# A one-token decode layer on one NeuronCore: the order of work written out, with weight chunks between the links of attention

## The chip, the cores and the metric

The kernel runs on 1 of the 8 cores of one Trainium2 chip. The metric is the time of one execution on the device in microseconds (us), the median of several runs. A core has a matrix engine (PE, with its weight loads listed apart as PEld), a vector engine (DVE), a scalar engine (ACT), a general engine (POOL) and a sync engine (SP), which here only issues DMAs. Each engine works through its own instructions in the order in which the program gives them, and waits where an instruction needs another engine's result. Sixteen DMA engines carry the data from the chip's memory into the core's own memory.

## The reference

One token `x` (1 x 1024) is normalised, and three things are added: `x` itself, attention over a window of 4096 cached keys and values (32 query heads that share 4 key/value heads), and a gated feed-forward layer. All is float32.

```python
def _A_ref(x, k_cache, v_cache, wq, wo):
    ...
    q = (lambda x, *d: x.transpose(*d))((x @ wq).reshape(B, Sq, Hq, Dh), 0, 2, 1, 3)
    k = jnp.repeat(k_cache[:, :, Sk - W:, :], rep, axis=1)
    v = jnp.repeat(v_cache[:, :, Sk - W:, :], rep, axis=1)
    scores = jnp.einsum("bhqd,bhkd->bhqk", q, k) * (Dh ** -0.5)
    p = _softmax(scores, axis=-1)
    o = jnp.einsum("bhqk,bhkd->bhqd", p, v)
    return (lambda x, *d: x.transpose(*d))(o, 0, 2, 1, 3).reshape(B, Sq, Hq * Dh) @ wo

def _B_ref(x, w_gate, w_up, w_down):
    g = jnp.einsum("bsd,df->bsf", x, w_gate)
    u = jnp.einsum("bsd,df->bsf", x, w_up)
    h = _gelu(g) * u
    return jnp.einsum("bsf,fd->bsd", h, w_down)
...
xn = _layernorm(x, axis=-1)
return x + _A_ref(xn, A_k_cache, A_v_cache, A_wq, A_wo) + _B_ref(xn, B_w_gate, B_w_up, B_w_down)
```

`wq` is 1024 x 4096, `wo` 4096 x 1024, `w_gate` and `w_up` 1024 x 3584, `w_down` 3584 x 1024. Every weight and every cached row in the window is read once, 94.4 MB in all, so the kernel is a stream of data with a little work on each piece.

## The kernel before

**The stream.** `items` is a list of 23 chunks: four of `wq` ("q"), then "k" 0, "g" 0 (`w_gate`), "v" 0, "g" 1 to 3, "k" 1, "u" 0 (`w_up`), "v" 1, "u" 1 to 3, four of `wo` ("o") and four of `w_down` ("d": eight tiles in each of the first three chunks, four in the last). A "k" or "v" chunk holds two key/value heads. `load(n)` takes one of the four buffers of the pool `stream` and issues the chunk's DMAs on SP's queue. The first four loads come ahead of all work; the load of chunk n+4 is written behind the work on chunk n, and waits on SP until every reader of that chunk's buffer is done. The last two chunks come in pieces (`TAIL`).

**The work on a chunk.** `project` (chunks q, g, u) multiplies each of a chunk's two rows by its element of `x` and adds it to `part` on DVE (`add_scaled`: line 191 for the first row of a matrix, line 193 for the others). At the end of a matrix, PE adds the 128 partitions of `part` together: `queries` for q, `projected` for g and u (line 212). `transpose_keys` turns a head's keys around with 32 PE transposes in eight groups of four (line 256), each group copied out by ACT to `kT` (line 257; two PSUM buffers alternate). `scores` multiplies (line 265), takes the maximum on DVE (`m`, line 268; `negm`, line 269) and the exponentials on ACT (line 271). `values` transposes the probabilities (lines 284 and 287) and multiplies with v (line 295; copied to `o_sb` on ACT, line 299). `maxima`, `factors`, `normalizers` and `heads` bring the four groups' maxima and sums together over a chain of small steps between PE, DVE and ACT (lines 308 to 354); its end is `oz`, the vector that `wo` is multiplied with. `gelu` (lines 365 to 371) and `hidden` (lines 375 and 376) do the same service for `w_down` and end in `hz`.

**The two output matrices.** `contract` walks over the tiles (128 rows x 1024) of a chunk of `wo` or `w_down`. Most go to DVE, which adds the scaled tile to `out_part` (line 193). The tiles in `ALONE`, 4 of the 32 of `wo` and 10 of the 28 of `w_down`, go to PE, four quarters of 256 columns each, into `out_p` (`accumulate`, line 384). Ahead of tile 26 of `w_down` (`MERGE`) PE adds `out_part` to `out_p`, so every DVE tile must be finished there; tiles 26 and 27 follow on PE. Then DVE adds `x` (line 448) and the result is stored.

**The order.** `tc.manual_schedule()` keeps the order of the program text on every engine. It comes from one loop over `items`: all work of chunk n, then the load of chunk n+4, then the work of chunk n+1. So in chunk "k" both heads' transposes and scores stand together, and the next weight chunk stands behind them in DVE's queue; `factors` stands behind `project` of u 1, `normalizers` and `heads` (as one piece) behind that of u 2, and `hidden` behind `projected("u")` and ahead of the tiles of o 0. In chunk "k" 1 the transposes of head 2 stand ahead of `projected("g")` and `gelu`.

Of the kernel before, what the change touches and what calls it, by code (L numbers as in the profile page):

```python
# [9 lines left out]
F32 = mybir.dt.float32  # L10
AF = mybir.ActivationFunctionType
# [4 lines left out]
P = 128  # L16
D = 1024
# [4 lines left out]
DF = 3584  # L22
NJ = D // (2 * P)
NB = 512
CO = D // 4
CF = DF // 4
TD = DF // P
GROUP = 8

TAIL = {0: 1, 1: 4}  # L30


ALONE = {"o": (0, 8, 16, 24), "d": (8, 12, 16, 18, 20, 22, 24, 25, 26, 27)}
MERGE = ("d", 26)
# [7 lines left out]
def tile_decode_layer(  # L42
# [28 lines left out]

    def grouped(w, a):
        return w[P * GROUP * a:min(P * GROUP * (a + 1), w.shape[0]), :].rearrange(
            "(p t) n -> p t n", p=P
        )

# [3 lines left out]
    items += [("o", a) for a in range(HQ // GROUP)]  # L80
    items += [("d", a) for a in range(-(-TD // GROUP))]
    source = {
        "q": lambda i: [paired(wq, i)], "g": lambda i: [paired(w_gate, i)], "u": lambda i: [paired(w_up, i)],
        "k": lambda i: [window(k_cache, 2 * i + g) for g in range(2)],
        "v": lambda i: [window(v_cache, 2 * i + g) for g in range(2)],
        "o": lambda i: [grouped(wo, i)], "d": lambda i: [grouped(w_down, i)],
    }
    loaded = {}

    def load(n):  # L90
        kind, i = items[n]
        chunk = stream.tile([P, STREAM], F32, name="chunk")
        at = 0
        for src in source[kind](i):
            size = math.prod(src.shape[1:])
            dst = chunk[:, at:at + size]
            at += size
            if len(src.shape) == 3:
                dst = dst.rearrange("p (t n) -> p t n", t=src.shape[1])
            step = TAIL.get(len(items) - 1 - n)  # L100
            if step:
                for t in range(0, src.shape[1], step):
                    cuts = 2 if n == len(items) - 1 and t == src.shape[1] - 1 else 1
                    for cut in range(cuts):
                        cols = slice(cut * D // cuts, (cut + 1) * D // cuts)
                        nc.sync.dma_start(dst[:, t:t + step, cols], src[:, t:t + step, cols])
            else:
                nc.sync.dma_start(dst, src)
        loaded[kind, i] = chunk
# [90 lines left out]

    def project(kind, jj, count):
        if jj == 0:
            part[kind] = work.tile([P, 8 * NB], F32, name="part", tag="part")
        w = loaded.pop((kind, jj))
        n = count * NB
        for r in range(2):
            add_scaled(
                part[kind][:, :n], w[:, r * n:(r + 1) * n], xz[:, r, jj, 0:1], jj == 0 and r == 0
            )

    def add_up(kind, c, at, w):
        nc.tensor.matmul(acc[kind][32 * c:32 * c + 32, at], unit, w, start=True, stop=True)  # L212


    def queries():
        acc["q"] = psum.tile([P, 2 * NB], F32, name="acc_q", tag="acc")
        w = part["q"].rearrange("p (h c s) -> p h c s", c=4, s=32)
        for b in range(2):
            for c in range(4):
                add_up("q", c, slice(b * NB, (b + 1) * NB), w[:, 16 * b:16 * b + 16, c, :])  # L220
# [4 lines left out]
        nc.vector.tensor_copy(  # L225
            qz[:, :, 0:REP], qT[:, :, 0].rearrange("p (g h) -> p g h", g=HKV)
        )

    def projected(kind):
        acc[kind] = psum.tile([P, 2 * NB], F32, name="acc_" + kind, tag="acc")
        full = DF // D * D
        w = part[kind][:, :full].rearrange("p (a c s i) -> p a c i s", a=DF // D, c=4, i=GROUP)
        rest = part[kind][:, full:DF].rearrange("p (c s i) -> p c i s", c=4, s=32)
        for c in range(4):
            add_up(kind, c, slice(0, NB), w[:, 0:2, c])
        for c in range(4):
            add_up(kind, c, slice(NB, NB + D // 4), w[:, 2, c])
        for c in range(4):  # L240
            add_up(kind, c, slice(NB + D // 4, DF // 4), rest[:, c])

# [59 lines left out]
    top = work.tile([HKV, 4, 32], F32, name="top")  # L302
    weight = work.tile([P, HKV], F32, name="weight")
    sel = same.rearrange("p c h -> p (c h)")

# [9 lines left out]
    def factors():  # L315
        mm_p = small("mm_p")
        nc.tensor.transpose(mm_p[:, :HKV], top.rearrange("g c h -> g (c h)"), ident[:HKV, :HKV])
        d = work.tile([P, HKV], F32, name="d")
        nc.vector.tensor_sub(d, m, mm_p[:, :HKV])
        e = work.tile([P, HKV], F32, name="e")  # L320
        nc.scalar.activation(e, d, AF.Exp, scale=SCALE)
        le = work.tile([P, HKV], F32, name="le")
        nc.vector.tensor_mul(le, l, e)
        return e, le

    def normalizers(e, le):
# [4 lines left out]
        nc.vector.tensor_mul(weight, e, r)  # L331

    def heads():
        w_p = small("w_p")
# [4 lines left out]
        for g in range(HKV):  # L339
            nc.scalar.activation(o_sb[:, g], o_sb[:, g], AF.Copy, scale=weight[:, g:g + 1])  # L340


        ot_p = small("ot_p")
        for c in range(4):
            nc.tensor.matmul(  # L345
                ot_p, pick[:, REP * c:REP * c + REP, :].rearrange("p h s -> p (h s)"),
                o_sb[:, :, c, :], start=(c == 0), stop=(c == 3),
            )
        own = work.tile([P, HKV, 16, 8], F32, name="own", tag="rows")
        nc.vector.tensor_mul(  # L350
# [8 lines left out]

    g_sb = work.tile([P, CF], F32, name="g_sb", tag="gate")  # L360
    h_sb = work.tile([P, CF], F32, name="h_sb")

    def gelu():
        t_sb = work.tile([P, CF], F32, name="t_sb", tag="rows")
        nc.scalar.activation(g_sb, acc["g"][:, :CF], AF.Copy)  # L365
        nc.vector.tensor_mul(t_sb, g_sb, g_sb)  # L366
# [7 lines left out]
    def hidden():  # L374
        nc.vector.tensor_mul(h_sb, g_sb, acc["u"][:, :CF])
        nc.vector.transpose(hz.rearrange("p t s -> p (t s)"), h_sb)


    out_p = psum.tile([P, CO], F32, name="out_p", tag="out")
    out_part = None  # L380

# [5 lines left out]

    def contract(kind, a, z, count):
        nonlocal out_part
        if kind == "o" and a == 0:  # L390
            out_part = work.tile([P, D], F32, name="out_part", tag="keys")
        w = loaded.pop((kind, a))
        for i in range(min(GROUP, count - GROUP * a)):
            t = GROUP * a + i
# [3 lines left out]
            if t in ALONE[kind]:  # L398
                accumulate(z[:, t, :], wt, kind == "o" and t == 0, kind == "d" and t == count - 1)
            else:  # L400
                add_scaled(out_part, wt, z[:, t, 0:1], kind == "o" and t == 1)

    ahead = 4
    for n in range(ahead):
        load(n)
    layer_norm()
    state = None
    for n, (kind, i) in enumerate(items):
        if kind == "q":
            project("q", i, 8)  # L410
        elif kind == "k":
            kn = loaded.pop(("k", i))
            half = STREAM // 2
            transpose_keys(2 * i, kn[:, :half])
            if i == 0:
                queries()
            else:
                projected("g")
                gelu()
            scores(2 * i)  # L420
            transpose_keys(2 * i + 1, kn[:, half:])
            scores(2 * i + 1)
        elif kind == "v":
            vn = loaded.pop(("v", i))
            half = STREAM // 2
            values(2 * i, vn[:, :half])
            values(2 * i + 1, vn[:, half:])
            if i == 1:
                maxima()
        elif kind in "gu":  # L430
            project(kind, i, DF // NB)
            if (kind, i) == ("u", 1):
                state = factors()
            elif (kind, i) == ("u", 2):
                normalizers(*state)
                heads()
        elif kind == "o":
            if i == 0:
                projected("u")
                hidden()  # L440
            contract("o", i, oz, HQ)
        else:
            contract("d", i, hz, TD)
        if n + ahead < len(items):
            load(n + ahead)

# [26 lines left out]
```

## Time and profile before

| | |
|---|---|
| time, median of 3 runs | 247.78 us (246.86 to 248.16) |
| the profiled execution: its time | 248.12 us |
| the profiled execution: its span (first to last instruction) | 246.3 us |
| read from memory | 94.38 MB |
| busy: DVE, PE, ACT | 173.8, 77.3, 35.9 us |

The span is what the views of the trace cover; the 1.8 us beside it is start and end of the execution. Below, the time is written from the start of the span. A row of the timeline gives start, duration, engine, line, operation, what is written and read with its shape, how many instructions are taken together, and in brackets how long the engine sat idle ahead of it and what ended that. A row of the windows gives a stretch, its length, the busy time (with the number of instructions) of PE, PEld, DVE, ACT and POOL, then the clock that PE was granted (1.00 is full), the share of the DMA engines and GB/s.

### The profile page before, as it was taken

The page shows a single profiled execution, that of the slowest core. Times are in us where ns is not written, and L with a number is a line of the kernel's source. Part 1 is how long each engine was busy: PE and PEld are TensorE (multiplying, and loading weights), DVE is VectorE, ACT ScalarE, POOL GpSimd, SP SyncE. Part 2 cuts the span into 40 slices and gives each one's busy share as a digit, 9 for nine tenths or more (in the row PEclk, how much of TensorE's full clock was granted, in tenths as well). Part 3 has the DMA queues.
Part 4 walks back from the last instruction along what each step waited for, and adds up shares of the span by engine and source line. Part 5 has one row for each costly group of instructions (what it writes and reads, how often), then busy time and mean ns, then how long its engine had stood idle before and what let it go on. Part 6 is the DMA issues. An engine that isn't in the chain of part 4 may idle for free.

```text
span 246.3 us, 1319 instructions
## 1 busy us (share of the span) xinstructions
PE 77.3 (31%) x492; PEld 38.8 (16%) x492; DVE 173.8 (71%) x128; ACT 35.9 (15%) x63; POOL 0.7 (0%) x6
## 2 busy tenths in 40 slices
PE   1000000395496100495296400370611000335004
PEld 1000000351362000342263100220200000101001
DVE  6285988932209999905419699229499999999990
ACT  2000000161644000153443100400000000000000
POOL 1000000000000000000000000000000000000000
PEclk9999999997779855599677955575695555557555
DMA  7999999999999999999999999999997999996000
GB/s 278 442 458 436 426 431 394 434 449 416 428 454 410 419 447 414 432 427 422 449 418 430 447 433 434 426 426 426 431 426 277 426 404 426 407 376 263 0 0 1
DMA packets 4782, 94.47 MB, mean 384 GB/s; under 512 B 540, under 2 KB 552, under 8 KB 1192
## 3 DMA queue, kind: packets, MB, share of 16 engines
q1 hardware_dynamic: 4760, 94.38, 90.2%
q8 instruction: 4, 0.07, 0.1%
q14 instruction: 2, 0.02, 0.0%
q10 hardware_dynamic: 16, 0.01, 0.0%
HBM read 94.38 MB, written 0.00 MB: 383 GB/s over the span
## 4 chain that ended last, share of the span: by engine, by line
DVE 43%; DMA 24%; PE 24%; ACT 5%; issue 2%; ACTq 0%; DVEq 0%
DVE out_part L193 24%; DMA chunk<-in_A_k_cache 19%; DVE part L193 11%; PE kt_p L256 9%; DMA chunk<-in_A_wq 5%; PE o_p L295 3%; PE s_p L265 3%; PE ot_p L345 2%; DVE m L268 2%; ACT p L271 2%; PE acc_u L212 1%; PE acc_g L212 1%; PE pt_p L284 1%; PE out_p L384 1%; DVE part L191 1%
## 5 line engine op out<-in xcount | busy, mean ns | idle before, releaser
L193 DVE SCALAR_TENSOR_TENSOR part<-chunk,xz,part 128x3584 f32<-128x3584 f32 (+1 forms) x21 | 86.7, 4128 | 5.0 <-DMA chunk<-in_A_wq 4.2
L256 PE MATMUL kt_p<-ident,chunk 128*128 128x128 f32 x128 | 25.0, 364 | 72.0 <-DMA chunk<-in_A_k_cache 61.0
L193 DVE SCALAR_TENSOR_TENSOR out_part<-chunk,oz,out_part 128x1024 f32<-128x1024 f32 x27 | 34.7, 1285 | 1.0
L256 PEld LDWEIGHTS kt_p<-ident,chunk 128*128 128x128 f32 x128 | 19.6, 187 | 79.7 <-DMA chunk<-in_A_k_cache 40.2
L257 ACT ACTIVATE kT<-kt_p 128x512 f32<-128x512 f32 x32 | 18.7, 597 | 68.2 <-PE kt_p L256 67.7
L193 DVE SCALAR_TENSOR_TENSOR out_part<-chunk,hz,out_part 128x1024 f32<-128x1024 f32 x18 | 23.1, 1285 | 0.6
L268 DVE TENSOR_REDUCE m<-s_p 128x1 f32<-128x1024 f32 x4 | 4.9, 1223 | 23.0 <-PE s_p L265 23.0
L384 PE MATMUL out_p<-chunk,hz 128*32 128x256 f32 x80 | 9.3, 609 | 27.8 <-DMA chunk<-in_B_w_down 27.8
L265 PE MATMUL s_p<-kT,qz 128*32 128x512 f32 x64 | 9.1, 694 | 2.6 <-DVE qz L225 2.6
L191 DVE TENSOR_SCALAR part<-chunk,xz 128x3584 f32<-128x3584 f32 (+1 forms) x3 | 6.5, 2169 | 4.5 <-DMA chunk<-in_A_wq 4.5
L295 PE MATMUL o_p<-chunk,pT 128*32 128x512 f32 x64 | 8.4, 644 | 4.1 <-ACT pT L287 4.1
L384 PEld LDWEIGHTS out_p<-chunk,hz 128*32 128x32 f32 x80 | 3.0, 155 | 34.3 <-issue 24.9
L345 PE MATMUL ot_p<-o_sb,pick 128*128 128x512 f32 x8 | 6.0, 917 | 2.8 <-ACT o_sb L340 2.8
L350 DVE TENSOR_TENSOR own<-ot_p,low 128x512 f32<-128x512 f32 x1 | 0.7, 692 | 8.6 <-PE ot_p L345 8.6
L212 PE MATMUL acc_u<-part,unit 128*32 128x512 f32 (+2 forms) x24 | 3.4, 718 | 9.7 <-DVE part L193 9.7
L366 DVE TENSOR_TENSOR t_sb<-g_sb 128x896 f32<-128x896 f32 x1 | 1.1, 1094 | 7.6 <-ACT g_sb L365 7.6
L384 PE MATMUL out_p<-chunk,oz 128*32 128x256 f32 x32 | 2.8, 447 | 10.1 <-DMA chunk<-in_A_wo 10.1
L271 ACT ACTIVATE p<-s_p,negm 128x1024 f32<-128x1024 f32 x4 | 4.5, 1114 | 8.9 <-DVE negm L269 8.9
L384 PE MATMUL out_p<-out_part,unit 128*32 128x256 f32 x8 | 1.1, 635 | 14.5 <-DVE out_part L193 14.5
L284 PE MATMUL pt_p<-ident,p 128*128 128x128 f32 x32 | 5.2, 317 | 0.0
L224 DVE STREAM_TRANSPOSE qT<-q_sb 128x1024 f32<-128x1024 f32 x1 | 1.2, 1245 | 5.2 <-ACT q_sb L222 5.2
L284 PEld LDWEIGHTS pt_p<-ident,p 128*128 128x128 f32 x32 | 4.1, 162 | 4.0 <-issue 4.0
(86 smaller groups left out, 51.1 us busy)
## 6 DMA issues: line engine op xcount, KB each, us to landing
chunk<-in_A_wq SPq DMA_DIRECT2D x4, 4096.0 KB, 30.8
chunk<-in_A_wo SPq DMA_DIRECT2D x4, 4096.0 KB, 22.4
chunk<-in_B_w_gate SPq DMA_DIRECT2D x4, 3584.0 KB, 16.6
chunk<-in_B_w_up SPq DMA_DIRECT2D x4, 3584.0 KB, 15.1
chunk<-in_A_k_cache SPq DMA_DIRECT2D x4, 2048.0 KB, 26.0
chunk<-in_A_v_cache SPq DMA_DIRECT2D x4, 2048.0 KB, 23.6
chunk<-in_B_w_down SPq DMA_DIRECT2D x2, 4096.0 KB
chunk<-in_B_w_down SPq DMA_DIRECT2D x2, 2048.0 KB, 12.1
```

The source lines that it names most:

```text
L191: nc.vector.tensor_scalar(total, w, factor, None, op0=ALU.mult)
L193: nc.vector.scalar_tensor_tensor(total, w, factor, total, op0=ALU.mult, op1=ALU.add)
L212: nc.tensor.matmul(acc[kind][32 * c:32 * c + 32, at], unit, w, start=True, stop=True)
L256: nc.tensor.transpose(t_p[:, jj * P:(jj + 1) * P], kn[:, j * DH:(j + 1) * DH], ident)
L257: nc.scalar.activation(kT[:, i, :], t_p, AF.Copy)
L265: nc.tensor.matmul(s_p[32 * c:32 * c + 32, b, :], qz[:, g, :], kT[:, i, :], start=True, stop=True)
L268: nc.vector.reduce_max(m[:, g:g + 1], s_p, axis=AX.XY)
L271: nc.scalar.activation(p, s_p, AF.Exp, bias=negm[:, g:g + 1], scale=SCALE, accum_out=l[:, g:g + 1])
L284: nc.tensor.transpose(t_p[:, jj * P:(jj + 1) * P], p[:, b, jj * P:(jj + 1) * P], ident)
L295: nc.tensor.matmul(o_p[32 * jj:32 * jj + 32, :, :], pT[:, b, jj].rearrange("p c h -> p (c h)"), v[:, b, jj], start=(b == 0), stop=(b == 1),)
L345: nc.tensor.matmul(ot_p, pick[:, REP * c:REP * c + REP, :].rearrange("p h s -> p (h s)"), o_sb[:, :, c, :], start=(c == 0), stop=(c == 3),)
L384: nc.tensor.matmul(out_p[32 * c:32 * c + 32, :], z, w[:, c * CO:(c + 1) * CO], start=start, stop=stop)
```

## The change

The loop over `items` is gone; every step is written out, with the loads at stated places. Chunks, buffers (four) and the order of the loads stay.

- **Order.** `queries` comes ahead of the transposes of head 0. g 0 is projected between `scores(0)` and the transposes of head 1, u 0 between `scores(2)` and the transposes of head 3. `projected("g")` and `gelu` come ahead of the transposes of head 2. `maxima` stands behind `scores(3)`, `factors` between the values of heads 2 and 3. `project` can take one row of a chunk: the first row of u 1 stands between `factors` and `normalizers`, the second row of u 1 and the first of u 2 between `scaled` (the first part of the old `heads`) and `heads` (its rest). The DVE tiles of o 0 stand ahead of `hidden`.
- **Tiles.** `w_down` is now four chunks of seven tiles (`DOWN`). Eight tiles (`WIDE`) go to PE in two halves of 512 columns into a new PSUM tile `wide_p`, which takes the place of `o_p`; nine (`QUARTERS`) go to PE in quarters as before. DVE keeps 27 of `wo` and 16 of `w_down` (28 and 18 before). `narrow`, behind chunk d 1, adds `wide_p` to `out_part` in two DVE operations on 32 partitions x 512.
- **Sums.** `projected` adds 8 blocks of 448 columns in place of 12 of 512, 256 and 128; `gelu` and `hidden` work on the same 896 columns, held as 2 x 448.
- **Pieces.** Chunks o 3, d 1 and d 2 come in two pieces, d 3 in six, the last of these in two halves (`PIECES`).

```diff
+PIECES = {("o", 3): (4, 4), ("d", 1): (3, 4), ("d", 2): (3, 4), ("d", 3): (2, 1, 1, 1, 1, 1)}
+WIDE = [("o", 0), ("o", 4), ("o", 8), ("o", 16), ("o", 24), ("d", 0), ("d", 7), ("d", 10)]
+QUARTERS = [("d", t) for t in (14, 16, 18, 20, 22, 24, 25, 26, 27)]
 MERGE = ("d", 26)
...
-        w = part[kind][:, :full].rearrange("p (a c s i) -> p a c i s", a=DF // D, c=4, i=GROUP)
...
+        w = part[kind][:, :DF].rearrange("p (a c s i) -> p a c i s", a=TD // DOWN, c=4, i=DOWN)
+        for b in range(2):
+            for c in range(4):
+                add_up(kind, c, (b, slice(0, CF)), w[:, 2 * b:2 * b + 2, c])
...
+            if (kind, t) in WIDE:
+                if (kind, t) == WIDE[0]:
+                    wide_p = psum.tile([P, NB], F32, name="wide_p", tag="o")
+                for c in range(2):
+                    nc.tensor.matmul(
+                        wide_p[32 * c:32 * c + 32, :], z[:, t, :], wt[:, c * NB:(c + 1) * NB],
+                        start=(kind, t) == WIDE[0], stop=(kind, t) == WIDE[-1],
+                    )
+            elif (kind, t) in QUARTERS:
+                accumulate(z[:, t, :], wt, (kind, t) == QUARTERS[0], (kind, t) == QUARTERS[-1])
...
+    def narrow():
+        for c in range(2):
+            rows, cols = slice(32 * c, 32 * c + 32), slice(c * NB, (c + 1) * NB)
+            nc.vector.tensor_add(out_part[rows, cols], out_part[rows, cols], wide_p[rows, :])
...
+    for _ in range(4):
+        load_next()
     layer_norm()
+    for i in range(NJ):
+        project("q", i)
+        load_next()
+    queries()
+    transpose_keys(0, cache("k", 0))
+    scores(0)
+    project("g", 0)
+    transpose_keys(1, cache("k", 1))
+    scores(1)
+    load_next()
+    load_next()
+    values(0, cache("v", 0))
+    values(1, cache("v", 1))
+    load_next()
+    for i in range(1, NJ):
+        project("g", i)
+        load_next()
+    projected("g")
+    gelu()
+    transpose_keys(2, cache("k", 2))
+    scores(2)
+    project("u", 0)
+    transpose_keys(3, cache("k", 3))
+    scores(3)
+    load_next()
+    load_next()
+    maxima()
+    values(2, cache("v", 2))
+    factors()
+    values(3, cache("v", 3))
+    load_next()
+    project("u", 1, (0,))
+    normalizers()
+    ot_p = scaled()
+    project("u", 1, (1,))
+    load_next()
+    project("u", 2, (0,))
+    heads(ot_p)
+    project("u", 2, (1,))
+    load_next()
+    project("u", 3)
+    load_next()
+    projected("u")
+    contract("o", 0)
+    hidden()
+    load_next()
+    for a in range(1, HQ // GROUP):
+        contract("o", a)
+        load_next()
+    for a in range(TD // DOWN):
+        contract("d", a)
+        if a == 1:
+            narrow()
```

More of the change, by code (lines that the diff above doesn't have):

```diff
@@ L99, in load @@
                 dst = dst.rearrange("p (t n) -> p t n", t=src.shape[1])
[L100 to L107, printed above, removed]
+            t = 0
+            for step in PIECES.get((kind, i), ()):
+                cuts = 2 if n == len(items) - 1 and t + step == DOWN else 1
+                for cut in range(cuts):
+                    cols = slice(cut * D // cuts, (cut + 1) * D // cuts)
+                    nc.sync.dma_start(dst[:, t:t + step, cols], src[:, t:t + step, cols])
+                t += step
+            if t == 0:
                 nc.sync.dma_start(dst, src)
@@ L199, in tile_decode_layer, with project @@
     acc, part = {}, {}
-    def project(kind, jj, count):
-        if jj == 0:
+    def project(kind, jj, rows=(0, 1)):
+        if jj == 0 and rows[0] == 0:
             part[kind] = work.tile([P, 8 * NB], F32, name="part", tag="part")
-        w = loaded.pop((kind, jj))
-        n = count * NB
-        for r in range(2):
+        w = loaded[kind, jj]
+        n = HQ * DH if kind == "q" else DF
+        for r in rows:
             add_scaled(
@@ L211, in add_up @@
     def add_up(kind, c, at, w):
-        nc.tensor.matmul(acc[kind][32 * c:32 * c + 32, at], unit, w, start=True, stop=True)
+        nc.tensor.matmul(acc[kind][(slice(32 * c, 32 * c + 32), *at)], unit, w, start=True, stop=True)
     def queries():
@@ L231, in projected @@
     def projected(kind):
-        acc[kind] = psum.tile([P, 2 * NB], F32, name="acc_" + kind, tag="acc")
-        full = DF // D * D
-        w = part[kind][:, :full].rearrange("p (a c s i) -> p a c i s", a=DF // D, c=4, i=GROUP)
[L235 to L241, printed above, removed]
+        acc[kind] = psum.tile([P, 2, NB], F32, name="acc_" + kind, tag="acc")
+        w = part[kind][:, :DF].rearrange("p (a c s i) -> p a c i s", a=TD // DOWN, c=4, i=DOWN)
+        for b in range(2):
+            for c in range(4):
+                add_up(kind, c, (b, slice(0, CF)), w[:, 2 * b:2 * b + 2, c])
     m = work.tile([P, HKV], F32, name="m")
@@ L303, in tile_decode_layer @@
     weight = work.tile([P, HKV], F32, name="weight")
+    e = work.tile([P, HKV], F32, name="e")
+    le = work.tile([P, HKV], F32, name="le")
     sel = same.rearrange("p c h -> p (c h)")
@@ L348, in heads @@
             )
+        return ot_p
+    def heads(ot_p):
         own = work.tile([P, HKV, 16, 8], F32, name="own", tag="rows")
@@ L357, in heads @@
         )
-    g_sb = work.tile([P, CF], F32, name="g_sb", tag="gate")
-    h_sb = work.tile([P, CF], F32, name="h_sb")
+    g_sb = work.tile([P, 2, CF], F32, name="g_sb", tag="gate")
+    h_sb = work.tile([P, 2, CF], F32, name="h_sb")
     def gelu():
-        t_sb = work.tile([P, CF], F32, name="t_sb", tag="rows")
-        nc.scalar.activation(g_sb, acc["g"][:, :CF], AF.Copy)
+        t_sb = work.tile([P, 2, CF], F32, name="t_sb", tag="rows")
+        nc.scalar.activation(g_sb, acc["g"][:, :, :CF], AF.Copy)
         nc.vector.tensor_mul(t_sb, g_sb, g_sb)
@@ L386, in accumulate, with contract @@
             )
[L388 to L394, printed above, removed]
+    def contract(kind, a):
+        nonlocal out_part, wide_p
+        size, z = (GROUP, oz) if kind == "o" else (DOWN, hz)
+        w = loaded[kind, a]
+        for i in range(size):
+            t = size * a + i
             wt = w[:, i * D:(i + 1) * D]
@@ L397, in contract @@
                 accumulate(unit, out_part, False, False)
-            if t in ALONE[kind]:
-                accumulate(z[:, t, :], wt, kind == "o" and t == 0, kind == "d" and t == count - 1)
-            else:
[L401 to L405, printed above, removed]
-    layer_norm()
[L407 to L445, printed above, removed]
@@ new lines, in contract @@
+            if (kind, t) in WIDE:
[5 more added lines that the diff above has]
+                        start=(kind, t) == WIDE[0], stop=(kind, t) == WIDE[-1],
+                    )
+            elif (kind, t) in QUARTERS:
+                accumulate(z[:, t, :], wt, (kind, t) == QUARTERS[0], (kind, t) == QUARTERS[-1])
+            else:
+                first = out_part is None
+                if first:
+                    out_part = work.tile([P, D], F32, name="out_part", tag="keys")
+                add_scaled(out_part, wt, z[:, t, 0:1], first)
```

41 lines of the change are left out of this document (23 added, 18 removed).

## The prediction

> **What bounds the kernel now.** I read the slices of the page first, then two stretches of the windows, then the waits, then DVE's timeline.
>
> ```profile
> DVE  6285988932209999905419699229499999999990
> DMA  7999999999999999999999999999997999996000
> GB/s 278 442 458 436 426 431 394 434 449 416 428 454 410 419 447 414 432 427 422 449 418 430 447 433 434 426 426 426 431 426 277 426 404 426 407 376 263 0 0 1
> 130.00:180.00 50.00, 18.42 (x98) 7.57 (x102) 34.42 (x21) 6.05 (x13) 0.00 (x0) 0.66 1.00 431
> 225.00:240.00 15.00, 0.64 (x8) 0.16 (x8) 14.61 (x12) 0.00 (x0) 0.00 (x0) 0.60 0.05 20
> ```
>
> Data flows at about 431 GB/s until the 37th slice of 6.16 us. Then for 15 us (225 to 240) hardly a byte moves, while DVE is full (14.61 of 15 us). So the end is a backlog on DVE. It arose earlier: the slices 9 to 11 and 18 to 27 show holes in DVE while data kept coming. Four groups of waits make most of the holes:
>
> ```profile
> DVE m L268 <- PE s_p L265: 23.0, 3, 10.5
> DVE own L350 <- PE ot_p L345: 8.6, 1, 8.6
> DVE t_sb L366 <- ACT g_sb L365: 7.6, 1, 7.6
> DVE h_sb L375 <- PE acc_u L212: 3.6, 1, 3.6
> ```
>
> (us in total, times, longest.) These are DVE's links in attention's chains, with the next weight chunk queued behind them.
>
> ```profile
> 97.03 7.94 DVE L193 SCALAR_TENSOR_TENSOR part<-chunk,xz,part 128x3584 f32<-128x3584 f32 x2 [0.30 <-DMA chunk<-in_B_w_gate]
> 166.40 7.93 DVE L193 SCALAR_TENSOR_TENSOR part<-chunk,xz,part 128x3584 f32<-128x3584 f32 x2
> 180.79 35.62 DVE L193 SCALAR_TENSOR_TENSOR out_part<-chunk,oz,out_part 128x1024 f32<-128x1024 f32 x27
> 216.45 23.74 DVE L193 SCALAR_TENSOR_TENSOR out_part<-chunk,hz,out_part 128x1024 f32<-128x1024 f32 x18
> 240.24 1.08 PE L384 MATMUL out_p<-out_part,unit 128*32 128x256 f32 x8 [14.53 <-DVE out_part L193]
> 241.10 1.93 PE L384 MATMUL out_p<-chunk,hz 128*32 128x256 f32 x16
> 243.10 0.42 DVE L448 TENSOR_TENSOR y<-out_p,x_out 128x256 f32<-128x256 f32 x1 [2.91 <-PE out_p L384]
> ```
>
> At 97.03 DVE waits for data: not a microsecond of the holes before it has survived. From 166.40 on DVE runs without a hole except 3.6 us (acc_u), up to 240.2. Then follow 24 matmuls, the sum and the store: 6.1 us to 246.3. So the end is DVE's last tile plus 6.1, and only what DVE saves behind 97 counts.
>
> **The change, part by part. Up to 105: nothing.** g 0 moves into the hole ahead of the second maximum, but g 1 to g 3 land when they did; g 3 landed at 97.0 and its 7.94 us set 105.0 in both. `queries` ahead of the transposes of head 0 may delay the first chain by a us or so.
>
> ```profile
> 73.39 1.22 DVE L268 TENSOR_REDUCE m<-s_p 128x1 f32<-128x1024 f32 x1 [10.51 <-PE s_p L265]
> ```
>
> That chain ended here at 74.6, and g 1 lands near 80 (97.0 less two chunks of 3.67 MB at 431 GB/s), so some 5 us of DVE's waiting for g 1 cover the delay. I price both at 0.
>
> **105 to `oz`: the chain.** Here nothing but the sum of links serves. The rows of before that give them:
>
> ```profile
> 108.19 3.41 PE L212 MATMUL acc_g<-part,unit 128*32 128x512 f32 x24
> 115.52 0.95 ACT L369 ACTIVATE h_sb<-t_sb 128x896 f32<-128x896 f32 x1 [2.95 <-DVE t_sb L368]
> 118.18 1.22 DVE L268 TENSOR_REDUCE m<-s_p 128x1 f32<-128x1024 f32 x1
> 120.78 1.07 ACT L257 ACTIVATE kT<-kt_p 128x512 f32<-128x512 f32 x2
> 128.51 1.23 DVE L268 TENSOR_REDUCE m<-s_p 128x1 f32<-128x1024 f32 x1 [8.93 <-PE s_p L265]
> 131.45 2.59 PE L295 MATMUL o_p<-chunk,pT 128*32 128x512 f32 x16 [2.03 <-ACT pT L287]
> 133.97 1.97 PE L284 MATMUL pt_p<-ident,p 128*128 128x128 f32 x8
> 135.87 1.95 PE L295 MATMUL o_p<-chunk,pT 128*32 128x512 f32 x16
> 156.08 2.56 ACT L340 ACTIVATE o_sb<-o_sb,weight 128x512 f32<-128x512 f32 x4 [9.22 <-DVE weight L338]
> 164.69 0.69 DVE L350 TENSOR_TENSOR own<-ot_p,low 128x512 f32<-128x512 f32 x1 [8.65 <-PE ot_p L345]
> ...
> 146.47 0.15 DVE L319 TENSOR_TENSOR d<-m,mm_p 128x4 f32<-128x4 f32 x1
> 155.26 0.59 PE L335 MATMUL w_p<-weight,spread 128*128 128x4 f32 x2 [7.49 <-DVE weight L331]
> ...
> L193 DVE SCALAR_TENSOR_TENSOR part<-chunk,xz,part 128x3584 f32<-128x3584 f32 x14 | 55.3, 3949 | 0.7 <-DMA chunk<-in_B_w_gate 0.3
> L191 DVE TENSOR_SCALAR part<-chunk,xz 128x3584 f32<-128x3584 f32 x2 | 4.2, 2076 | 0.0
> ```
>
> (The last two rows are groups: busy us, mean ns of one.)
>
> From the start of acc_g to the end of the tanh before: 108.19 to 116.47, 8.28 us; now from 105.0, so 113.3. The copies of head 2's keys stand behind the tanh on ACT, so PE stops after two groups; from the first copy to the maximum took 7.73 (120.78 to 128.51): the maximum starts at 121.0 (before 118.18, so this move loses 2.8). `m` and `negm` end at 122.4, and u 0 fills DVE: 2.08 + 3.95, to 128.5. Beside it head 3 runs: 2.60 from maximum to first copy, 7.73 to its maximum, which starts at 131.35 and is done at 132.8. Of u 0's 6.0 us all is hidden; 2.9 us of hole stay ahead of this maximum. Then come the moved links, at which DVE waits for everything: from maximum to the product with v 2.94, to 134.3; the product 2.59, to 136.9; `factors` (transpose 0.2, `d` 0.15, ACT's copy of `o_sb` 0.6 that stands ahead of `e`, 0.21, `le` 0.16) to 138.0. Here 4.5 us of hole are new: before, u 1 stood ahead of `d` and hid it. Row 0 of u 1 runs 138.0 to 142.0. Beside it the values of head 3 take PE 3.85 (133.97 to 137.82), to 141.0, and `normalizers`' matmul 0.6 more. `r`, `weight`, the matmul of 0.6 and the copy end at 143.2, with 0.7 us of hole. From there to `own` took 8.61 (156.08 to 164.69), so 151.85; row 1 of u 1 and row 0 of u 2 fill 7.95 of it. `own` and the sum behind it take 1.8: `oz` is done at 153.65, and u 2's second row and u 3 remain; before, 166.4 with u 3 alone. Gain 12.75 - 3.96 = **8.8 us**.
>
> **From `oz` to the end on DVE.** u: 3.96 + 7.94 = 11.9. Then `o` 0 needs no acc_u, so the 3.6 us hole goes: PE's 3.5 us lie beside six tiles, 7.3 us. Tiles: 27 + 16 = 43 for 46; 0.75 for the first, 42 x 1.32 (35.62 / 27) = 55.4. `hidden` 2.2 as before. `narrow` is not in the trace: the nearest row is `own`, 512 columns out of PSUM on 128 partitions, 0.69; on 32 partitions I take the same, twice with the step between, 1.45; it can't be below 0.3 (two instructions of 0.15, as `d`) and I keep 0.3 to 1.5. The sum is 71.7, so DVE ends at **225.35**; 153.65 + 71.7. Against 240.2 these are 8.8 + 3.6 + 3 x 1.32 - 1.45 = 14.9 us.
>
> **PE's tiles** lie beside DVE. A tile in quarters took PE 0.97 (1.93 for 16 matmuls); a wide tile uses two column groups in place of four, at most twice that, 1.95, and one comes in 9 us. The nine quartered tiles of the last two chunks arrive every 1.2 us, so PE holds them. The 24 matmuls behind the last DVE tile took 2.83 with the clock at 0.50; I keep that.
>
> ```profile
> 225.07 0.64 PE L384 MATMUL out_p<-chunk,hz 128*32 128x256 f32 x8 [0.21 <-DMA chunk<-in_B_w_down]
> 225.00:226.00 1.00, 0.64 (x8) 0.16 (x8) 0.96 (x2) 0.00 (x0) 0.00 (x0) 1.00 0.53 205
> 240.00:242.00 2.00, 1.76 (x20) 0.85 (x24) 0.19 (x1) 0.00 (x0) 0.00 (x0) 0.50 0.00 0
> ```
>
> Eight of them took 0.64 at clock 1.00, so 24 might take 1.9. The Trainium skill's page "TensorE: Matmul & The Clock Gate", section "Part 1: The HAM clock gate", says that the clock rises after a busy window of about 3.4 us and falls after an idle one; this trace agrees in kind (0.50 after 14.5 us of idling). By that rule the busier PE of the new tail could be warm there, and the sum would be 0.9 us less.
>
> **The sums of `projected`** stream the same 7168 columns (both passes of 896 in four groups); only the step between them goes from 8 to 7 elements. Nearest row: 3.41. If the step no longer slowed it, acc_q is the bound:
>
> ```profile
> 53.44 1.92 PE L212 MATMUL acc_q<-part,unit 128*32 128x512 f32 x16
> 58.01 3.33 PE L265 MATMUL s_p<-kT,qz 128*32 128x512 f32 x16 [2.64 <-DVE qz L225]
> ```
>
> 8192 columns without a step in 1.92, so 1.7 us could be gained on the chain; I take 0.
>
> **The data.** The last data bounds everything from below.
>
> ```profile
> 188.74 0.33 SPq L108 DMA_DIRECT2D chunk<-in_B_w_down  x1
> 188.00:189.00 1.00, 0.00 (x0) 0.00 (x0) 0.96 (x2) 0.00 (x0) 0.00 (x0) 0.50 0.00 0
> 189.47 1.08 PE L384 MATMUL out_p<-chunk,oz 128*32 128x256 f32 x8 [9.07 <-DMA chunk<-in_A_wo]
> 102.02 6.25 PE L256 MATMUL kt_p<-ident,chunk 128*128 128x128 f32 x32 [20.83 <-DMA chunk<-in_A_k_cache]
> ```
>
> The last of `wo` landed at 189.5, and d 0 was issued only at 188.74, when `o` 0 was read: 0 GB/s around 188, some 2.7 us lost up to 195. Now `o` 0's DVE tiles end at 166.3 + 7.3 = 172.9 or so, and d 0 is issued there, far ahead. So d's 14.68 MB (28 tiles of 128 x 1024 x 4 bytes) follow 189.5 at 431 GB/s: 223.5, and 0.8 for the slower small pieces (400 GB/s in the last slices): 224.3. Every load's wait on SP shifts too: k 1's buffer comes free after head 3's transposes, near 129.4 (126.5 before), v 1's at 141.0 (137.9), u 2's at 157.6 (154.9). Counted back from 189.5, u 1 lands at 133.5, u 3 at 150.5, `o` 1 at 170: each issue still comes ahead of the data's end, u 2's with the least margin, about 3 us. SP has nothing else queued that matters.
>
> **The sum.** DVE 225.35, PE 2.83, `y`, store and steps 3.3: span 231.5; with the 1.8 us beside the span, **233.3** against 248.1 of that execution, which lies 0.3 above the median of 247.78. I let 233.3 stand.
>
> **The rivals. The data sets the end.** If the chain from 105 to `oz` is 1.7 us shorter (projected) and the tail warm, DVE is done when the last half tile lands: 224.3 + 0.64 + 3.3 + 1.8 = 230.0. For it: only 1 us between 225.35 and 224.3. Against it: every link would have to fall to the good side. **A colder chain.** PE idles between links more than before; the product with v took 1.95 or 2.59, and 16 such matmuls at a clock of 0.58 took 3.33 (scores at 58.01). With both products there, and the same again in the transposes and the next sums, 3 to 5 us: 236 to 238. **The holes are not filled**: a piece of weight work stands in front of a link that is ready, and delays it by as much as it fills. Then the 8.8 us are gone and 242.1 stays. Against it: in the sum above each piece is shorter than the link beside it (6.0 under 8.9, 7.95 under 8.6). **Slower than before: the stream starves.** Four buffers, and k 1's is held until head 3's transposes end; each us that these end beyond about 132 is a us without data, and u 2, behind which `heads` now stands, lands later by it. To pass 249 the end must be 15.7 us later, and DVE's waiting for u 2 (landing 142.0, needed 147) hides 5 more: the transposes would have to end near 153 instead of 129.4. Nothing in the rows comes near that.
>
> **How the numbers follow.** Forecast (230.5 to 235.5) 0.69; data sets the end (229 to 230.5) 0.14; colder chain (235.5 to 239) 0.10; holes not filled (242) 0.03; starved, over 249, 0.03; another place within 0.5%, 0.01. The range reaches from 229 to 238: it takes in the bounds of `projected`, `narrow`, the clock and the products. Some 0.5%, 1.2 us, is what a measurement of this kernel tells from no change. Faster 0.95, same 0.02, slower 0.03.
>
> **What would show it.** Right: no hole at acc_u; `m` of head 2 near 121, `le` near 138, `oz` near 153.7; no slice near 277 GB/s; DVE's last tile near 225, a us behind the last data. Wrong: a row of DVE idle for DMA after 166, `oz` beyond 160, or SP issuing u 2 after 133.

## The result, and the profile after

The time fell from 247.67 us (median of 6 runs, 246.04 to 248.16) to **232.37 us** (median of 6, 231.08 to 232.93): a ratio of 0.9385, 95% interval 0.9346 to 0.9424. The profiled execution took 232.93 us with a span of 231.0. Forecast: 233.3 us, range 229 to 238.

The slices of the page, after; line numbers have moved by a few, so line 196 is `add_scaled`, 385 `accumulate`, 402 the wide tiles, 417 `narrow`:

```profile
DVE  6275989882291298892708539979999999999990
PEclk9999999999967995555759799575596555555555
DMA  7999999899999999999999999999999999999950
GB/s 273 455 431 397 443 454 454 380 426 472 399 416 465 402 457 412 421 418 444 416 440 425 437 413 422 466 420 420 443 437 406 426 433 431 424 424 427 403 224 1
```

A slice is 5.78 us now. The slice with 277 GB/s is gone, and so is the long stretch in which DVE was full and no byte moved: data flows into the 39th slice of 40. DVE still has holes in slices 10 to 14 (all but 12) and 19 to 24. DVE's timeline says which (start, duration, and in brackets the idle time before it):

```profile
74.38 1.23 DVE L265 TENSOR_REDUCE m<-s_p 128x1 f32<-128x1024 f32 x1 [4.72 <-PE s_p L262]
75.64 0.15 DVE L266 TENSOR_SCALAR negm<-m 128x1 f32<-128x1 f32 x1
80.14 7.94 DVE L196 SCALAR_TENSOR_TENSOR part<-chunk,xz,part 128x3584 f32<-128x3584 f32 x2 [4.34 <-DMA chunk<-in_B_w_gate]
...
97.23 7.94 DVE L196 SCALAR_TENSOR_TENSOR part<-chunk,xz,part 128x3584 f32<-128x3584 f32 x2 [0.58 <-DMA chunk<-in_B_w_gate]
...
121.91 1.23 DVE L265 TENSOR_REDUCE m<-s_p 128x1 f32<-128x1024 f32 x1 [6.58 <-PE s_p L262]
...
132.16 1.23 DVE L265 TENSOR_REDUCE m<-s_p 128x1 f32<-128x1024 f32 x1 [2.86 <-PE s_p L262]
...
137.80 0.16 DVE L320 TENSOR_TENSOR le<-l,e 128x4 f32<-128x4 f32 x1 [0.44 <-ACT e L319]
...
151.89 0.69 DVE L349 TENSOR_TENSOR own<-ot_p,low 128x512 f32<-128x512 f32 x1 [1.22 <-PE ot_p L339]
152.62 1.07 DVE L353 TENSOR_REDUCE oz<-own 128x32 f32<-128x512 f32 x1
153.60 11.92 DVE L196 SCALAR_TENSOR_TENSOR part<-chunk,xz,part 128x3584 f32<-128x3584 f32 x3
165.43 0.75 DVE L194 TENSOR_SCALAR out_part<-chunk,oz 128x1024 f32<-128x1024 f32 x1
...
172.70 1.08 DVE L374 TENSOR_TENSOR h_sb<-g_sb,acc_u 128x896 f32<-128x896 f32 x1
...
217.14 1.37 DVE L417 TENSOR_TENSOR out_part<-out_part,wide_p 32x512 f32<-32x512 f32 x2
218.55 6.57 DVE L196 SCALAR_TENSOR_TENSOR out_part<-chunk,hz,out_part 128x1024 f32<-128x1024 f32 x5
228.03 0.42 DVE L490 TENSOR_TENSOR y<-out_p,x_out 128x256 f32<-128x256 f32 x1 [2.91 <-PE out_p L385]
```

What the reader is to see: up to 97.23 DVE waits for data (4.34 and 0.58 us), so 105.2 is set by the stream, as before. `oz` is done at 153.69 (before: 166.49, but with one u chunk left in place of one and a half). Ahead of `h_sb` there is no idle time. From 153.6 on DVE never stops, and its last tile ends at 225.12 in place of 240.2. Then come, as before, 24 matmuls, the sum and the store:

```profile
225.17 1.08 PE L385 MATMUL out_p<-out_part,unit 128*32 128x256 f32 x8 [2.30 <-DVE out_part L196]
226.02 1.93 PE L385 MATMUL out_p<-chunk,hz 128*32 128x256 f32 x16
```

PE had waited 2.30 us for DVE. In the last us ahead of those matmuls no byte moved, while DVE was full:

```profile
222.00:224.00 2.00, 0.86 (x8) 0.00 (x0) 1.93 (x3) 0.00 (x0) 0.00 (x0) 0.50 0.36 136
224.00:225.00 1.00, 0.00 (x0) 0.00 (x0) 1.00 (x1) 0.00 (x0) 0.00 (x0) 0.50 0.00 0
```

So DVE's backlog, not the data, still sets the end of this kernel, by a little. The stages give the gain: 240.2 - 225.1 = 15.1 us on DVE's last tile, 15.3 in the span.

### The profile page after: what moved, and what is told of

The parts are those of the page before. It is cut to its first block, busy times and chain, and to the rows that moved or that the text cites. A ratio compares the mean times of both kernels' runs of the same rounds, so it can differ in the third digit from the quotient of the medians.

```text
span 231.0 us, 1280 instructions
## 1 busy us (share of the span) xinstructions
PE 85.5 (37%) x468; PEld 36.8 (16%) x468; DVE 171.3 (74%) x127; ACT 35.1 (15%) x63; POOL 0.7 (0%) x6
## 4 chain that ended last, share of the span: by engine, by line
DVE 43%; DMA 28%; PE 19%; ACT 5%; issue 3%; SPq 1%; ACTq 0%; DVEq 0%
DVE out_part L196 24%; DMA chunk<-in_A_wq 17%; DVE part L196 14%; DMA chunk<-in_B_w_gate 11%; PE kt_p L253 8%; PE s_p L262 3%; PE ot_p L339 3%; ACT kT L254 2%; DVE m L265 2%; PE acc_q L215 2%; PE acc_g L215 2%; PE out_p L385 1%; ACT p L268 1%; PE o_p L292 1%; ACT o_sb L336 1%
## 5 line engine op out<-in xcount | busy, mean ns | idle before, releaser
L196 DVE SCALAR_TENSOR_TENSOR out_part<-chunk,oz,out_part 128x1024 f32<-128x1024 f32 x26 | 33.4, 1283 | 0.9
L196 DVE SCALAR_TENSOR_TENSOR out_part<-chunk,hz,out_part 128x1024 f32<-128x1024 f32 x16 | 20.6, 1285 | 0.6
L215 PE MATMUL acc_q<-part,unit 128*32 128x512 f32 x16 | 3.6, 1058 | 44.2 <-DVE part L196 44.2
L215 PE MATMUL acc_g<-part,unit 128*32 128x448 f32 x16 | 3.4, 987 | 23.1 <-DVE part L196 23.1
L402 PE MATMUL wide_p<-chunk,hz 128*32 128x512 f32 x12 | 5.8, 1059 | 16.2 <-DMA chunk<-in_B_w_down 16.2
L402 PE MATMUL wide_p<-chunk,oz 128*32 128x512 f32 x20 | 6.6, 781 | 11.3 <-DMA chunk<-in_A_wo 11.3
L215 PE MATMUL acc_u<-part,unit 128*32 128x448 f32 x16 | 3.4, 991 | 13.7 <-DVE part L196 13.7
L225 ACT ACTIVATE q_sb<-acc_q 128x1024 f32<-128x1024 f32 x1 | 1.0, 1025 | 47.5 <-PE acc_q L215 47.5
L262 PE MATMUL s_p<-kT,qz 128*32 128x512 f32 x64 | 8.2, 634 | 0.0
L364 ACT ACTIVATE g_sb<-acc_g 128x896 f32<-128x896 f32 x1 | 0.9, 917 | 25.9 <-PE acc_g L215 25.9
```

What stands on the lines that cost most here:

```text
L196: nc.vector.scalar_tensor_tensor(total, w, factor, total, op0=ALU.mult, op1=ALU.add)
L215: nc.tensor.matmul(acc[kind][(slice(32 * c, 32 * c + 32), *at)], unit, w, start=True, stop=True)
L262: nc.tensor.matmul(s_p[32 * c:32 * c + 32, b, :], qz[:, g, :], kT[:, i, :], start=True, stop=True)
L402: nc.tensor.matmul(wide_p[32 * c:32 * c + 32, :], z[:, t, :], wt[:, c * NB:(c + 1) * NB], start=(kind, t) == WIDE[0], stop=(kind, t) == WI ...
```

## The experiments

Four theories stood against each other. **A**: the end is DVE's last tile plus six us, so a change counts by what it does to DVE behind 105 us, after the holes that are left have taken their part. **B**: the data sets the end, and the gain came from a stream that no longer starves. **C**: the tiles on PE and the smoother stream made the larger part of the gain. **D**: each filled hole is worth its length. The medians below stand against the 232.4 us of the changed kernel; each ratio is against the kernel before, timed on the same chip. The intervals of the ratios are 0.7 to 1.8 us to either side, so the times alone do not decide about single microseconds; for those the traces are read.

**Three tiles back to DVE.**

```diff
-WIDE = [("o", 0), ("o", 4), ("o", 8), ("o", 16), ("o", 24), ("d", 0), ("d", 7), ("d", 10)]
+WIDE = [("o", 0), ("o", 8), ("o", 16), ("o", 24), ("d", 10)]
```

> Three tiles (o 4, d 0, d 7) go back from PE to DVE, so DVE has 46 as before the change; order and all else as after the change. Theory A (the end is DVE's last tile plus 6 us): DVE's last tile ends 3 x 1.32 = 4.0 us later, 229.1 in place of 225.1, and the time is 232.4 + 4.0 = 236.4 us. Rival B (the data sets the end, and the gain came from the stream that no longer starves): DVE has slack, 232.4 to 233.5 us.

Measured: 235.57 us, ratio 0.9542 (0.9485 to 0.9600), so +3.2. In its trace DVE's timeline ends thus:

```profile
150.65 1.07 DVE L353 TENSOR_REDUCE oz<-own 128x32 f32<-128x512 f32 x1
...
220.54 6.57 DVE L196 SCALAR_TENSOR_TENSOR out_part<-chunk,hz,out_part 128x1024 f32<-128x1024 f32 x5
```

From `oz` (151.72) to the last tile (227.11) it took 75.39 us; in the changed kernel 71.43 (153.69 to 225.12). The difference is 3.96, the price of the three tiles to the hundredth. The median shows 0.8 less, and in this execution the chain ahead of `oz` was done 2.0 us sooner; that spread has its place in the last section. By the ratios (0.9542 against 0.9385) the difference is 3.9. Theory A holds, B falls: it gave 233.5 us at most.

**`hidden` ahead of `o` 0.**

```diff
     projected("u")
-    contract("o", 0)
     hidden()
+    contract("o", 0)
```

> hidden goes back ahead of the tiles of o 0. Theory A: DVE waits again for the sums of u (3.45 us on PE, and the step from engine to engine), a hole of 3.6 us as before the change, and nothing later takes it up: 232.4 + 3.6 = 236.0 us. Rival B (data sets the end): under 233.5 us.

Measured: 235.45 us, ratio 0.9556 (0.9481 to 0.9630), +3.1. By the ratios it is 4.2; theory A gave 3.6. The hole is back in DVE's timeline, at its old length:

```profile
167.33 1.09 DVE L374 TENSOR_TENSOR h_sb<-g_sb,acc_u 128x896 f32<-128x896 f32 x1 [3.62 <-PE acc_u L215]
```

**The old order with the new tiles.** The loop over `items` (24 chunks, not 23: 4 + 6 + 6 + 4 + 4) came back (all work of a chunk, then the next load), with the tiles, pieces and sums of the change.

> The order of before (the loop over chunks) with the tiles, pieces and sums of after. Theory A: of the gain only the three tiles less narrow stay, 3 x 1.32 - 1.4 = 2.6 us: 247.7 - 2.6 = 245.1 us, with the hole of 8.6 us ahead of own and that of 3.6 us ahead of h_sb back in DVE. Rival C (the tiles on PE and the smoother stream make the larger part): under 240 us.

Measured: 244.56 us (7 runs), ratio 0.9898 (0.9857 to 0.9938).

```profile
163.26 0.69 DVE L349 TENSOR_TENSOR own<-ot_p,low 128x512 f32<-128x512 f32 x1 [8.07 <-PE ot_p L339]
163.99 1.07 DVE L353 TENSOR_REDUCE oz<-own 128x32 f32<-128x512 f32 x1
...
176.49 1.09 DVE L374 TENSOR_TENSOR h_sb<-g_sb,acc_u 128x896 f32<-128x896 f32 x1 [3.59 <-PE acc_u L215]
...
229.74 6.57 DVE L196 SCALAR_TENSOR_TENSOR out_part<-chunk,hz,out_part 128x1024 f32<-128x1024 f32 x5
```

Both holes of before stand there again, and theory C, which gave less than 240 us, falls. So the tiles, with the pieces and sums, are worth some 3 us (247.87 - 244.56 = 3.3 on that chip, 2.5 by the ratio, expected 2.6), the order the other 12. The traces divide it alike. DVE's last tile ends here at 236.31, 3.9 ahead of before: 2.45 of this lie behind `oz`, where the tiles are, and 1.4 ahead of it, where `oz` is done at 165.06 in place of 166.49; no run takes these 1.4 us apart. The order then brings the last tile forward by another 11.2 us, to 225.12.

**u 0 behind both heads.**

```diff
-    project("u", 0)
     transpose_keys(3, cache("k", 3))
     scores(3)
+    project("u", 0)
```

> The projection of u 0 goes from between the two heads' scores to behind both; all else as after the change. Theory A (DVE's order counts, with the holes that are left): u 0's 6.0 us fall on the time behind the second maximum, where after has a hole of 3.3 us (2.8 ahead of d, 0.4 ahead of le) that it fills instead: 232.4 + 6.0 - 2.9 = 235.5 us, and d near 140.4. Rival D (each piece of weight work is worth its length): 232.4 + 6.0 = 238.4 us. Rival B (data sets the end): no change.

Measured: 235.40 us, ratio 0.9522 (0.9484 to 0.9561): +3.0, not +6.0.

```profile
131.75 1.23 DVE L265 TENSOR_REDUCE m<-s_p 128x1 f32<-128x1024 f32 x1 [8.77 <-PE s_p L262]
...
140.12 0.16 DVE L318 TENSOR_TENSOR d<-m,mm_p 128x4 f32<-128x4 f32 x1 [0.42 <-PE mm_p L316]
```

The hole ahead of the maximum grows from 2.86 to 8.77, u 0's length. But the next one, ahead of `d`, shrinks from 2.80 to 0.42, for the chain runs on through PE while DVE does u 0 there. Theory A had named 235.5, with `d` near 140.4. Filling a hole of 6 was worth 3, because the work would otherwise have filled the one behind it. This is where theory D, which gave 238.4, falls.

**g 0 behind both heads.**

```diff
-    project("g", 0)
     transpose_keys(1, cache("k", 1))
     scores(1)
     load_next()
+    project("g", 0)
     load_next()
```

> The projection of g 0 goes back behind both heads' scores; all else as after the change. Theory A (up to 105 the data sets the pace, so filling that hole was worth nothing): g 0 runs from about 75.5 to 81.5 and g 1 follows a us and a half behind its landing at 80.1; g 2 and g 3 take that back while DVE waits less for data, and the third chunk ends near 105.2 as now: 232.4 us, within 0.5%. Rival D (each filled hole is worth its length): 232.4 + 4.7 = 237 us or more.

Measured: 233.19 us, ratio 0.9436 (0.9393 to 0.9480), an interval that overlaps that of the changed kernel. DVE ran g 0 to g 3 without waiting for data:

```profile
78.19 27.88 DVE L196 SCALAR_TENSOR_TENSOR part<-chunk,xz,part 128x3584 f32<-128x3584 f32 x7
```

It ended at 106.07, 0.9 later than 105.17. That is what filling this hole bought in the traces: 6.0 us of work moved, 0.9 us gained (0.8 by the medians, 1.3 by the ratios). Theory A named 0, theory D 4.7 or more.

**Whole chunks in place of halves.**

```diff
-    project("u", 1, (0,))
+    project("u", 1)
+    load_next()
     normalizers()
     ot_p = scaled()
-    project("u", 1, (1,))
-    load_next()
-    project("u", 2, (0,))
-    heads(ot_p)
-    project("u", 2, (1,))
+    project("u", 2)
     load_next()
+    heads(ot_p)
```

> u 1 and u 2 are projected whole: u 1 ahead of normalizers, u 2 between the two parts of heads, no halves. Theory A: what counts is that one chunk's 7.9 us lie beside the 9 us link from weight to own; two halves or one whole chunk is the same. The link starts 3.9 us later and ends near 155.8, but then only u 3 is left: 232.4 us, within 0.5%. Rival D (the halves shorten the chain): the 3.9 us come back, 236.3 us.

Measured: 232.80 us, ratio 0.9420 (0.9370 to 0.9471): no difference that these runs can tell. `own` comes at 155.74 with 0.78 us of hole, but then only u 3 is left:

```profile
155.74 0.69 DVE L349 TENSOR_TENSOR own<-ot_p,low 128x512 f32<-128x512 f32 x1 [0.78 <-PE ot_p L339]
...
165.29 0.75 DVE L194 TENSOR_SCALAR out_part<-chunk,oz 128x1024 f32<-128x1024 f32 x1
```

DVE begins with `wo` at 165.29 against 165.43. These two times alone do not settle it, since head 3's maximum came at 130.70 here and at 132.16 there, and the product with v behind it took 3.51 us on PE here and 1.92 there. From the end of `le` to the first tile of `wo`, the stretch that the edit touches, the two agree: 27.30 us here (137.99 to 165.29), 27.55 there (137.88 to 165.43). What counts is that 7.9 us of weight work lie beside the 9 us link to `own`, not how they are cut.

**Three ways on from there.** More tiles to PE:

```diff
+WIDE = [("o", 0), ("o", 4), ("o", 8), ("o", 12), ("o", 16), ("o", 20), ("o", 24), ("o", 28), ("d", 0), ("d", 7), ("d", 10)]
```

> Three more tiles (o 12, o 20, o 28) go from DVE to PE in wide halves, 40 stay on DVE. Theory A has a floor close by: DVE's last tile would end at 221.2, but in the profile of after PE ends tile 25 at 222.9, and the merge and tiles 26 and 27 take 2.8 us behind that: end 2.3 us earlier and no more, 230.1 us. Without a floor (DVE alone decides) it would be 4.0 us less, 228.4. Rival B (data already sets the end): 232 to 232.5, no change.

The merge behind tile 27, in `contract` and at the end of the loop over d:

```diff
-            if (kind, t) == MERGE:
-                accumulate(unit, out_part, False, False)
...
+    accumulate(unit, out_part, False, True)
```

> The merge of out_part goes behind tile 27, so that tiles 26 and 27 no longer wait for DVE. Theory A: behind DVE's last tile there are 8 matmuls (1.1 us) in place of 24 (2.8): 232.4 - 1.75 = 230.6 us. Rival B (data sets the end): no change, or slower by the 1.1 us of the merge that then stand behind the data.

The keys of head 2 ahead of the sums of g:

```diff
-    projected("g")
-    gelu()
     transpose_keys(2, cache("k", 2))
     scores(2)
+    projected("g")
+    gelu()
```

> The transposes and scores of head 2 go back ahead of the sums of g and gelu (they stood there before the change). Theory A: the maximum of head 2 comes at 110.3 in place of 121.9, the hole of 6.6 us ahead of it goes, that of head 3 comes near 126.4 in place of 132.2, and u 1 starts when it lands, near 133.4, in place of 137.9: DVE is done 4.5 us earlier, at 220.6, and PE's last tiles then set the end as with more wide tiles: 230.1 us. If the chain costs what it did: 232.4 us.

Measured: 230.05 us, ratio 0.9310 (0.9267 to 0.9352), with more wide tiles; 230.50, ratio 0.9319 (0.9288 to 0.9350), with the merge last; 230.01, ratio 0.9314 (0.9272 to 0.9355), with the keys first. Each lies within 0.1 us of what theory A gave (230.1, 230.6, 230.1), closer than the intervals of the ratios could have promised. With more wide tiles DVE is done early, at 220.80, and PE goes on from tile 25 into the merge without a pause, so PE's last blocks set the end there:

```profile
214.23 6.57 DVE L196 SCALAR_TENSOR_TENSOR out_part<-chunk,hz,out_part 128x1024 f32<-128x1024 f32 x5
221.72 1.08 PE L385 MATMUL out_p<-chunk,hz 128*32 128x256 f32 x8 [0.21 <-DMA chunk<-in_B_w_down]
222.57 1.08 PE L385 MATMUL out_p<-out_part,unit 128*32 128x256 f32 x8
```

With the keys first it is the same: DVE's last tile ends at 221.34, and PE's merge starts at 222.89, right behind tile 25. DVE's timeline with the keys first shows that the part of the change which put `gelu` ahead of the keys cost time:

```profile
110.58 1.23 DVE L265 TENSOR_REDUCE m<-s_p 128x1 f32<-128x1024 f32 x1 [5.44 <-PE s_p L262]
...
126.24 1.22 DVE L265 TENSOR_REDUCE m<-s_p 128x1 f32<-128x1024 f32 x1
...
133.74 3.95 DVE L196 SCALAR_TENSOR_TENSOR part<-chunk,xz,part 128x3584 f32<-128x3584 f32 x1 [1.70 <-DMA chunk<-in_B_w_up]
```

Head 2's maximum comes 11.3 us earlier (110.58 for 121.91), head 3's without a hole, and u 1 now waits for its data.

**All together**, with tile 23 of `w_down` on PE and the merge ahead of tile 24:

```diff
+QUARTERS = [("d", t) for t in (14, 16, 18, 20, 22, 23, 24, 25, 26, 27)]
+MERGE = ("d", 24)
```

> Keys of head 2 first, tiles o 12 and o 20 on PE too, tile d 23 on PE in quarters, and the merge ahead of tile 24. Theory A: DVE's last tile (d 21) ends near 219.2, by its data; PE then has six blocks of 0.86 us from 219.1 on and ends with the data, near 224.2, against 224.9 with more wide tiles alone: 229.2 to 229.5 us. If a floor other than PE's last tiles holds: 230.0 us as with more wide tiles.

Measured: 229.99 us (6 runs, 229.76 to 230.19), ratio 0.9296 (0.9268 to 0.9323). It beats both kernels, and missed its expectation of 229.2 to 229.5 us by 0.5 to 0.8; the expectation had named 230.0 for the case of a floor other than PE's tiles. It is no faster than more wide tiles or the keys first alone. PE's weight loads at the end tell why:

```profile
221.78 0.20 PEld L385 LDWEIGHTS out_p<-chunk,hz 128*32 128x32 f32 x8 [0.66 <-DMA chunk<-in_B_w_down]
223.04 0.16 PEld L385 LDWEIGHTS out_p<-chunk,hz 128*32 128x32 f32 x8 [1.06 <-DMA chunk<-in_B_w_down]
223.66 0.14 PEld L385 LDWEIGHTS out_p<-chunk,hz 128*32 128x32 f32 x4 [0.47 <-DMA chunk<-in_B_w_down]
224.31 0.14 PEld L385 LDWEIGHTS out_p<-chunk,hz 128*32 128x32 f32 x4 [0.50 <-DMA chunk<-in_B_w_down]
```

Tiles 25, 26 and both halves of 27 are each waited for; the last half is there at 224.31, and 0.67 us later the sum starts. I had put PE's end at 224.2, with the data, and left out the last half's own work behind its arrival. So here the stream sets the end, with its bytes and its pieces as they are; other pieces at the end of the stream were not tried.

## Why the prediction was right

The end on DVE: predicted 225.35 for its last tile, measured 225.12 in the profiled execution. By its steps:

- **Up to 105: nothing.** Measured: the first chain was later by 1.0 us (the second maximum at 74.38 for 73.39): the transposes of head 0 now stand behind the sums of q, and these took 3.64 us in place of 1.92 (see the last section). DVE's wait for g 1 (4.34 us, I had said some 5) hid it. With g 0 moved back the third chunk ended 0.9 us later, so a cover of nearly everything, not of all.
- **The chain to `oz`:** 153.65 predicted, 153.69 measured, but by two errors that cancel. From the first copy of head 2's keys to its maximum it took 8.47 us where I had used the 7.73 of before, as PE ran the transposes and scores more slowly; so the maxima of heads 2 and 3 were later than I said (121.91 for 121.0, 132.16 for 131.35). The product with v took 1.92 where I had used the 2.59 of before, so `le` came at 137.96 for 138.0. That it fits to the hundredth is luck in another way too: the profiled executions of three of the experiments, which run the same program up to there, had `oz` done at 151.72, 151.88 and 151.93, a fourth (the merge last) at 153.16.
- **`hidden` behind `o` 0:** 3.6 us predicted, hole of 3.62 when undone. **Tiles:** 3.96 predicted, 3.96 on the trace when undone. **`narrow`:** 1.45 taken, 1.37 measured; 32 partitions took the time of 128.
- **The sums of `projected`:** no gain was counted for the smaller step of their operand, and none came: 3.43 us, before 3.41.
- **The tail:** from the first of the 24 matmuls to `y` it took 2.86 us (225.17 to 228.03), as before (240.24 to 243.10). PE's clock was 0.50 there, so the 0.9 us that a clock of 1.00 would have given did not come.
- **The data:** last landing predicted 224.3, seen at 224.31 where a kernel waits for it. The rival in which the data sets the end was priced at 230.0, and 229.99 is where the kernel with everything together stands. In the changed kernel DVE's last tile came 0.8 us behind that time, so the rival lost narrowly.
- **The stream:** u 2's issue was predicted near 129.4, with 3 us to spare; SP issued at 129.94, and no starving followed:

```profile
129.94 0.80 SPq L111 DMA_DIRECT2D chunk<-in_B_w_up  x2
172.85 0.33 SPq L111 DMA_DIRECT2D chunk<-in_B_w_down  x1
```

  d 0 went out at 172.85 (predicted 172.9, before 188.74). The 166.3 from which the prediction adds this up already has the first of the six tiles in it; it is 165.6 + 7.3.

What the prediction had at the wrong size is small: the span came out at 231.0 for 231.5, of which DVE's last tile makes 0.2 and the end behind `y` (2.55 us from the end of `y`, before 2.78) 0.2. In the reading of the slices of before, the holes reach to slice 12, the emptiest, and not to 11; the hole in it, 10.51 us ahead of a maximum, was counted.

## What to carry to other kernels

Where one engine's backlog sets the end, add up its holes only behind the last place where it waited for data; holes ahead of that place are nearly free (here 0.9 us came of 6.0). Work put into a hole is worth what the next holes would not have taken of it: 6 us of work moved forward gained 3 in one place and about 1 in another. And price the floor of the stream (last byte, last tile, store) beside the sum, since it tells which improvements can add up: here three kinds of step, each worth 1.9 to 2.4 us alone, came to 2.4 together.

## What the runs showed of the hardware

**The spread of the chain goes with PE's clock.** In the windows, after (first two rows) and with more wide tiles (last two), of the same work in the same order:

```profile
105.00:109.00 4.00, 3.78 (x18) 0.95 (x19) 0.17 (x1) 0.28 (x1) 0.00 (x0) 0.50 0.95 407
114.00:119.50 5.50, 5.42 (x24) 4.42 (x24) 1.29 (x2) 3.50 (x7) 0.00 (x0) 0.50 1.00 426
```

```profile
105.00:109.00 4.00, 3.83 (x20) 0.99 (x21) 0.11 (x1) 0.31 (x1) 0.00 (x0) 0.64 0.99 424
114.00:119.50 5.50, 5.46 (x32) 3.96 (x36) 1.25 (x2) 3.94 (x7) 0.00 (x0) 0.69 1.00 426
```

With a mean clock of 0.50 in both stretches PE did 24 transposes in the second where it did 24 and eight matmuls of the scores with 0.64 and 0.69, and the maximum of head 2 came at 121.91 against 120.67. The instructions are the same; what differs is the clock. Over the six executions of the changed kernel the mean granted clock orders the spans too: 231.0 and 230.7 us at 0.745, 230.2, 229.7 and 229.6 at 0.751, 229.1 at 0.757. The executions of the kernel before show no such order. The Trainium skill's page "TensorE: Matmul & The Clock Gate", section "Part 1: The HAM clock gate", says that the window which decides this runs freely and does not start with the kernel; the traces fit, but no run here was made to show it. In the profiled executions of the first two experiments `oz` came some 2 us sooner too, which fits medians below what the trace of their edit adds up to; that it is the reason is not shown.

**A busy PE is not always at full clock.** In the changed kernel's tail the clock stayed at 0.50 though PE was busy for 4.31 of 7 us; with everything together, where PE ran on nearly without a pause from 217.94, it rose to 1.00 behind 222. The first row is the changed kernel, the others are everything together:

```profile
215.00:222.00 7.00, 4.31 (x36) 1.19 (x40) 6.74 (x7) 0.00 (x0) 0.00 (x0) 0.50 1.01 404
215.00:222.00 7.00, 5.80 (x52) 1.99 (x56) 4.43 (x4) 0.00 (x0) 0.00 (x0) 0.50 1.01 402
222.00:223.00 1.00, 0.62 (x9) 0.00 (x0) 0.00 (x0) 0.00 (x0) 0.00 (x0) 0.88 0.46 164
223.00:224.00 1.00, 0.96 (x12) 0.30 (x12) 0.00 (x0) 0.00 (x0) 0.00 (x0) 1.00 0.15 55
```

**Sums over a stepped operand don't follow the clock, and one time does not fit the clock's record.** The sums of g took 3.41 us before, the clock at 1.00, and 3.43 now, the clock at 0.50 in the window above; the step of their operand was 8 and is 7 elements. The experiment with the old order takes the two apart: there the step is 7 and the clock 1.00, and they took 3.41. The sums of q, whose operand has no step, took 1.92 us before, right behind transposes; now they are PE's first work after 44 us of idling:

```profile
51.19 3.64 PE L215 MATMUL acc_q<-part,unit 128*32 128x512 f32 x16 [44.23 <-DVE part L196]
```

```profile
51.20:55.00 3.80, 3.80 (x17) 0.82 (x18) 0.00 (x0) 0.11 (x1) 0.00 (x0) 1.00 0.97 415
```

They took 3.64 us, 1.9 times as long, as if at half the clock, while the record of that stretch reads 1.00. Every other run in which they come first has them at 3.45 to 3.64, and the old order at 1.92. Whether the record or the reading is wrong there stays open. It cost nothing here, since DVE waited for g 1 anyway.
